# First chunk of attention and two gated MLPs: attention steps written ahead of the gates, one conversion step dropped, loads in another order

## The chip, the cores and the metric

One core of a Trainium2 chip runs the whole program. The metric is the device time of one execution in microseconds; the kernel before took 1794.08 us (median of three runs, 1793.94 to 1794.53).

## What is computed

Pooled attention feeds two MLPs:

```
k_p, v_p = mean of 8 neighbouring keys / values         # 576 -> 72
attn     = softmax(q @ k_p.T / sqrt(64)) @ v_p           # 8 batches, 8 heads, head size 64
x        = attn as [4608, 512]
x        = (sigmoid(x @ w_gate) * (x @ w_val)) @ w_out   # inner size 1536
out      = ((x @ w2_in) * cos(x @ w2_in)) @ w2_out       # inner size 2048
```

The weights arrive as float64 and are turned into two float32r parts on the chip, a high and a low one. A product of two such numbers is three matmuls: high times high, high times low, low times high.

## The kernel before

**Chunks.** The 4608 tokens are worked in nine chunks of 512. A chunk of the first stage is attention for its tokens, which gives xT (x transposed, high and low part), and then twelve blocks f = 0 to 11 of 128 gate and value columns (`gv_step`): 12 matmuls into a PSUM bank pg for the gate, 12 into pv for the value, a sigmoid on ScalarE (ACT), a product on VectorE (DVE, line 609), a store of g by DMA. After all chunks come the second product of the first MLP and the second MLP. That part, the larger, is not touched. In the code `c` is the chunk; chunk 0 is the one in which the weights are also converted.

**Order.** Every engine runs its instructions strictly in the order in which the code writes them. Nothing reorders them; the engines meet only where one waits for another's result. SyncE (SP) issues all DMAs in one queue, in order.

**Attention.** A tile of queries (up to 128 rows) goes through `q_step` (PE transposes q, ACT copies it to qT), `s_step` or, in the first half of chunk 0, `s_first` (PE multiplies with kbd, the pooled keys in block form; DVE takes the maxima mx; ACT the exponentials e and, in `s_first`, their sums sm), `normal` (DVE: a = e / sum, lines 529 to 540), `a_step` (PE transposes a into pa and par; ACT copies the high part to aT and aR; DVE subtracts for the low part, "aT low" and "aR low", line 66), and `x_step` (PE multiplies with the pooled values into px, ACT and DVE make xT's two parts). The scale 1 / (8 sqrt(64)) is put on in the exponential, and in `s_first` by an extra instruction on the negated maximum (line 512). GpSimd (POOL) pools the keys and values of the next chunk (`kv_pool`, line 362); `k_step` transposes the pooled keys into kbd, `v_step` prepares the values.

**The first chunk** is written out by hand from line 1133 on. Its four tiles are called by their first row: 0, 128, 256, 384. Its blocks 0, 1 and 2 are worked in two halves of 256 tokens: the first half while attention of the second is still under way (`gv_step(0, 0, 0)` is chunk 0, block 0, half 0), the second half at f = 0, 1, 2 of the loop in line 1244.

**Conversion.** A raw block goes through four steps: an exponent step on ACT (line 143), bit work on DVE (lines 148 and 153), the high part on ACT (line 161), the low part on DVE (line 66 with out wg or wv, "gate low", "value low"). `split()` (line 300) advances all of this by one stage for two raw tensors, a gate and a value block; the counters in `done` say how far each stage is. It only sees what has been loaded (`len(raws)`). In the first chunk `split()` stands before each block, and with two raw tensors a call the low parts of block f + 1 are made in the call before block f. Eight raw tensors (blocks 0 to 3) are loaded ahead of the loop, the other sixteen at the end of f = 0 by `load_all` (line 1274).

**The plan.** `plan(c)` spreads attention of chunk c over the twelve blocks of chunk c - 1; for chunk 1 the keys are loaded at f = 0 (line 676) and the values at f = 3 and pooled at f = 4 (lines 677 and 679). `kvraw` has two buffers, shared by keys and values, `kvrest` one.

**Banks.** PSUM tiles come from two rings of four banks, "t" and "g"; a new tile waits until the one four places before it has been read. Scores of `s_first` and the blocks share ring "g", all else uses "t".

Of the kernel before, what the change touches and what calls it, by code (L numbers as in the profile page):

```python
# [13 lines left out]
AF = mybir.ActivationFunctionType  # L14
ALU = mybir.AluOpType
# [8 lines left out]
def attention_two_mlps(  # L24
# [107 lines left out]

    def load_all():
        while len(raws) < min(len(order), len(slots) - AHEAD):
            load()
# [265 lines left out]
    def k_step(b):  # L401

        main, rest = kv["k"]
        pm = bank("t", [KM, NP, P], f"pk{b}")
        pr = bank("t", [KM, KM], f"pkr{b}")
        for i in range(NP):
            nc.tensor.transpose(pm[:, i], main[:, i], ident)
        nc.tensor.transpose(pr, rest[:KM, 0], ident[:KM, :KM])
        prv = pr.rearrange("d (i z y) -> d i z y", z=2, y=KR)
        for z in range(2):  # L410
            rows = kbds[b % 2][z * D:(z + 1) * D]
            nc.vector.tensor_copy(rows[:, :, z * KEYS:z * KEYS + KM], pm[:, :, z * KM:(z + 1) * KM])
            nc.vector.tensor_copy(rows[:, :, z * KEYS + KM:(z + 1) * KEYS], prv[:, :, z])

# [52 lines left out]
    def s_step(t):  # L467
# [4 lines left out]
        for g in range(2):  # L472
# [13 lines left out]
            half = e[:, 4 * g:4 * g + 4]  # L486
            nc.scalar.activation(half, half, AF.Exp, scale=1.0 / (POOL * math.sqrt(D)))
        sm = at.tile([rows, 16], F32, tag="sm", name=f"sm{b}_{s0}", bufs=2)[:, :H]
# [5 lines left out]
    def s_first(t, between=None):  # L494
# [7 lines left out]
        for g in range(2):  # L502
# [6 lines left out]
            m = mx[:, 4 * g:4 * g + 4]  # L509
            factor = 1.0 / (POOL * math.sqrt(D))  # L510
            nc.vector.reduce_max(out=m, in_=p, axis=AX.X)
            nc.vector.tensor_scalar(out=m, in0=m, scalar1=-factor, scalar2=None, op0=ALU.mult)
            scores.append(p)
        if between:
            between()
        for g, p in enumerate(scores):
            for h in range(4):
                n = 4 * g + h
                nc.scalar.activation(  # L519
                    e[:, n], p[:, h], AF.Exp, bias=mx[:, n:n + 1], scale=factor,  # L520
                    accum_out=sm[:, n:n + 1],
                )
# [67 lines left out]

    def gv_step(c, f, half=None):
        cols = slice(0, C) if half is None else slice(half * C // 2, (half + 1) * C // 2)
# [3 lines left out]
        for kind in "gv":  # L596
            w = block(kind, f)
            p = bank("g", [P, n], f"p{kind}{c}_{f}_{cols.start}")
            for kb in range(KB):
# [3 lines left out]
                nc.tensor.matmul(p, wl, x[:, 0, kb], start=False, stop=kb == KB - 1)  # L603
            pg.append(p)
        g = halves.pop(f, None)
        if g is None:
# [46 lines left out]
    def plan(c):  # L653
# [20 lines left out]
        if c < B:  # L674
            for g in range(3):
                (put_early if g < 2 else put)(NF - 2 if g < 2 else 0, kv_load, k, c, "k", g)
                put(3, kv_load, v, c, "v", g)
                put(1 if g == 2 or c == 1 else 0, kv_pool, c, "k", g, nc.gpsimd)
                put(4, kv_pool, c, "v", g, nc.gpsimd)
        order_ = []  # L680
# [450 lines left out]
    with tc.manual_schedule():  # L1131
# [44 lines left out]
        for n in range(2, 4):  # L1176
            stage_high(n)
        rest.append(s_first(first[3]))
        for n in range(2, 4):
            stage_low(n)  # L1180
        done.update(exponent=4, bits=4, high=4, parts=4)
        rest[2](nc.vector)
        gv_step(0, 0, 0)
        a_step(first[2])
        rest[3](nc.vector)
        split()
        gv_step(0, 1, 0)
        a_step(first[3])
        split()
        for i in range(KB):  # L1190
            x_step(0, 1, i, 1)
        split()
        gv_step(0, 2, 0)


# [25 lines left out]
        for c in range(NC):  # L1221
# [22 lines left out]
            for at_f, f in enumerate(FOLDED if c else range(NF)):  # L1244
                tick()
                if c == 0:
                    split()
                elif last:
# [25 lines left out]
                if c == 0 and at_f == 0:  # L1274
                    load_all()
                tock()
# [111 lines left out]
```

## Time and profile before

| | us |
|---|---|
| timed runs, median of 3 | 1794.08 (1793.94 to 1794.53) |
| the profiled execution | 1790.58 |
| its span, first to last instruction | 1788.6 |
| PE busy in it | 1751.2 (98%) |
| PE weight loads | 1469.0 (82%) |
| DVE busy | 1116.9 (62%) |
| ACT busy | 911.6 (51%) |
| POOL busy | 536.9 (30%) |

The shares are means over very different stages. The page's slices show PE at 9 tenths or more in all but the first two of forty, so the first 90 us are where PE has room, and it is there and a little behind it that the change lies. In the timelines below, a number in brackets at a row's end is how long the engine had been idle before that row and what ended the wait. The granted clock says at what share of its full 2.4 GHz the TensorE clock ran over a stretch; the other level is 1.2 GHz.

### The profile page before, as it was taken

What the parts mean: (1) busy time and instruction counts of PE and PEld (TensorE: products, weight loads), DVE (VectorE), ACT (ScalarE), POOL (GpSimd) and SP (SyncE); (2) the same over time, 40 slices, a digit from 0 to 9 for tenths busy, and PEclk for the clock granted to TensorE, in tenths of its full rate; (3) what the DMA queues carried; (4) which work ended last, traced back from release to release, by engine and by line L of the source; (5) the groups of instructions that cost most, each with busy time, mean ns of one, the idle gap of its engine ahead of it and who ended that gap; (6) DMA issues with size and microseconds to landing.
All of it is one profiled execution on the core that took longest, in us unless ns stands there. A gap on an engine that the chain in (4) does not pass through costs nothing. (4 is left out here: it accounts for less than half of the span.)

```text
span 1788.6 us, 24639 instructions
## 1 busy us (share of the span) xinstructions
PE 1751.2 (98%) x8560; PEld 1469.0 (82%) x8560; DVE 1116.9 (62%) x1830; ACT 911.6 (51%) x1528; POOL 536.9 (30%) x656
## 2 busy tenths in 40 slices
PE   5899999999999999999999999999999999999999
PEld 5778888888888888887888888888887878888887
DVE  7875565656565554456766765776766665655664
ACT  6654454545444453336555555565555544444443
POOL 4114444454545322220013443333334440000000
PEclk8999999999999999999999999999999999999999
DMA  9625565565866655958877778778738797666664
GB/s 270 201 72 165 190 199 183 168 183 165 251 205 210 199 193 192 338 188 277 273 252 256 260 248 262 247 248 266 257 111 289 252 330 266 216 214 212 218 218 147
DMA packets 291740, 397.47 MB, mean 222 GB/s; under 512 B 54560, under 2 KB 231200, under 8 KB 291616
## 3 DMA queue, kind: packets, MB, share of 16 engines
q1 hardware_dynamic: 291616, 395.91, 67.9%
q8 instruction: 67, 1.10, 0.3%
q14 instruction: 57, 0.47, 0.1%
HBM read 242.22 MB, written 153.62 MB: 221 GB/s over the span
## 5 line engine op out<-in xcount | busy, mean ns | idle before, releaser
L609 DVE TENSOR_TENSOR g<-pv,g 128x512 f32<-128x512 f32 (+1 forms) x111 | 75.1, 676 | 274.5 <-issue 125.2
L908 PE MATMUL ph<-x,wi 128*128 128x512 f32 x576 | 224.6, 390 | 1.9 <-DVE r L924 1.9
L909 PE MATMUL ph<-x,wi 128*128 128x512 f32 x576 | 224.3, 389 | 0.0
L910 PE MATMUL ph<-x,wi 128*128 128x512 f32 x576 | 224.1, 389 | 0.0
L914 DVE SCALAR_TENSOR_TENSOR r<-n,ph 128x512 f32<-128x512 int32 x144 | 98.9, 687 | 194.9 <-issue 87.3
L920 ACT ACTIVATE r<-r 128x512 f32<-128x512 f32 x144 | 91.2, 633 | 241.4 <-DVE r L917 98.8
L942 POOL TENSOR_TENSOR s<-r,r 128x256 f32<-128x256 f32 x64 | 75.4, 1179 | 434.9 <-DVE r L924 320.5
L66 DVE TENSOR_TENSOR sp<-sf,sp 128x1024 fp32r<-128x1024 f32 x112 | 132.8, 1229 | 80.9 <-ACT sp L998 80.9
L601 PE MATMUL pg<-xT,wg 128*128 128x512 f32 (+1 forms) x444 | 179.0, 403 | 1.8 <-ACT e L519 1.8
L603 PE MATMUL pg<-xT,wg 128*128 128x512 f32 (+1 forms) x444 | 172.4, 388 | 3.0 <-DVE wg L66 3.0
L602 PE MATMUL pg<-xT,wg 128*128 128x512 f32 (+1 forms) x444 | 172.0, 387 | 0.0
L603 PE MATMUL pv<-xT,wv 128*128 128x512 f32 (+1 forms) x444 | 170.9, 385 | 0.0
L601 PE MATMUL pv<-xT,wv 128*128 128x512 f32 (+1 forms) x444 | 170.7, 384 | 0.0
L602 PE MATMUL pv<-xT,wv 128*128 128x512 f32 (+1 forms) x444 | 170.6, 384 | 0.0
L998 ACT CAST sp<-sf 128x1024 fp32r<-128x1024 f32 x112 | 112.5, 1054 | 68.3 <-PE py_B L1101 25.0
L608 ACT ACTIVATE g<-pg 128x512 f32<-128x512 f32 (+1 forms) x111 | 65.1, 587 | 138.1 <-PE pg L603 88.4
L908 PEld LDWEIGHTS ph<-x,wi 128*128 128x128 f32 x576 | 108.3, 188 | 25.4 <-DVE r L924 2.7
L909 PEld LDWEIGHTS ph<-x,wi 128*128 128x128 f32 x576 | 108.3, 188 | 22.5
L910 PEld LDWEIGHTS ph<-x,wi 128*128 128x128 f32 x576 | 108.2, 188 | 22.5
L1096 PE MATMUL py_A<-tc,sp 128*128 128x512 f32 x384 | 120.6, 395 | 0.0
L917 DVE SCALAR_TENSOR_TENSOR r<-n,r 128x512 f32<-128x512 int32 x144 | 108.2, 751 | 5.0
L66 DVE TENSOR_TENSOR up<-uf,up 128x1024 fp32r<-128x1024 f32 x84 | 102.4, 1219 | 12.0 <-ACT up L819 12.0
(178 smaller groups left out, 4076.0 us busy)
## 6 DMA issues: line engine op xcount, KB each, us to landing
sf<-sd SPq DMA_DIRECT2D x112, 512.0 KB
so<-so SPq DMA_DIRECT2D x84, 512.0 KB
uf<-od SPq DMA_DIRECT2D x168, 256.0 KB
sd<-s SPq DMA_DIRECT2D x64, 512.0 KB
wo<-wo SPq DMA_DIRECT2D x56, 512.0 KB
od<-tg SPq DMA_DIRECT2D x48, 512.0 KB
sd<-r SPq DMA_DIRECT2D x64, 256.0 KB
raw_o<-in_moe_w_out_dram SPq DMA_DIRECT2D x28, 512.0 KB
```

Of the source, the lines that this page charges most:

```text
L66: engine.tensor_tensor(out=lo, in0=x, in1=hi.bitcast(F32), op=ALU.subtract)
L601: nc.tensor.matmul(p, wh, x[:, 0, kb], start=kb == 0, stop=False)
L602: nc.tensor.matmul(p, wh, x[:, 1, kb], start=False, stop=False)
L603: nc.tensor.matmul(p, wl, x[:, 0, kb], start=False, stop=kb == KB - 1)
L908: nc.tensor.matmul(p, wh, x[kb][:, 0], start=kb == 0, stop=False)
L909: nc.tensor.matmul(p, wh, x[kb][:, 1], start=False, stop=False)
L910: nc.tensor.matmul(p, wl, x[kb][:, 0], start=False, stop=kb == KB - 1)
L914: nc.vector.scalar_tensor_tensor(out=r, in0=n, scalar=-C1, in1=p, op0=ALU.mult, op1=ALU.add)
L917: nc.vector.scalar_tensor_tensor(out=r, in0=n, scalar=-C2, in1=r, op0=ALU.mult, op1=ALU.add)
L920: nc.scalar.activation(r, r, AF.Sin, scale=0.5)
L998: nc.scalar.copy(t[:, 0, h * w:(h + 1) * w], got[c, n, h])
L1096: nc.tensor.matmul(p, x[:, 0, m, s], w, start=fresh and m == 0, stop=False, skip_group_check=True,)
```

## The change

It has five parts.

1. The scale is multiplied into kbd when the keys are written there (`k_step`, copies become TENSOR_SCALARs); the maximum is negated by the reduction itself, so the extra instruction of `s_first` goes, and the exponentials have no scale.
2. `gv_step(..., later=True)` writes only the matmuls and returns the rest (`gated`: sigmoid and product), which the caller writes later. In the first chunk, `rest[2]` (`normal` of tile 256) stands before the low parts of block 1, `a_step` of tiles 256 and 384 before the sigmoids of blocks 0 and 1.
3. A `split()` is added at the end of the written-out part, and the `split()` at f = 5 of chunk 0 is left out.
4. The sixteen loads at the end of f = 0 are issued with the keys of chunk 1 behind the first six and the values of chunk 1 behind twelve; before, the keys stood ahead of all and the values were loaded at f = 3.
5. Chunk 1's values are pooled at f = 2 instead of f = 4.

```diff
--- before.py
+++ after.py
@@ -130,8 +130,8 @@
             raws.append(t)
         return t
 
-    def load_all():
-        while len(raws) < min(len(order), len(slots) - AHEAD):
+    def load_upto(n):
+        while len(raws) < n:
             load()
 
     def words(n, dtype, which):
@@ -409,8 +409,11 @@
         prv = pr.rearrange("d (i z y) -> d i z y", z=2, y=KR)
         for z in range(2):
             rows = kbds[b % 2][z * D:(z + 1) * D]
-            nc.vector.tensor_copy(rows[:, :, z * KEYS:z * KEYS + KM], pm[:, :, z * KM:(z + 1) * KM])
-            nc.vector.tensor_copy(rows[:, :, z * KEYS + KM:(z + 1) * KEYS], prv[:, :, z])
+            for o, i in ((rows[:, :, z * KEYS:z * KEYS + KM], pm[:, :, z * KM:(z + 1) * KM]),
+                         (rows[:, :, z * KEYS + KM:(z + 1) * KEYS], prv[:, :, z])):
+                nc.vector.tensor_scalar(
+                    out=o, in0=i, scalar1=1.0 / (POOL * math.sqrt(D)), scalar2=None, op0=ALU.mult
+                )
 
     def v_step(b, engine):
 
@@ -484,7 +487,7 @@
                 op=ALU.subtract,
             )
             half = e[:, 4 * g:4 * g + 4]
-            nc.scalar.activation(half, half, AF.Exp, scale=1.0 / (POOL * math.sqrt(D)))
+            nc.scalar.activation(half, half, AF.Exp)
         sm = at.tile([rows, 16], F32, tag="sm", name=f"sm{b}_{s0}", bufs=2)[:, :H]
         for g in range(2):
             h = slice(4 * g, 4 * g + 4)
@@ -507,9 +510,7 @@
                     x[:, 2 * g + i], kbds[b % 2][:, 2 * g + i], start=True, stop=True,
                 )
             m = mx[:, 4 * g:4 * g + 4]
-            factor = 1.0 / (POOL * math.sqrt(D))
-            nc.vector.reduce_max(out=m, in_=p, axis=AX.X)
-            nc.vector.tensor_scalar(out=m, in0=m, scalar1=-factor, scalar2=None, op0=ALU.mult)
+            nc.vector.reduce_max(out=m, in_=p, axis=AX.X, negate=True)
             scores.append(p)
         if between:
             between()
@@ -517,7 +518,7 @@
             for h in range(4):
                 n = 4 * g + h
                 nc.scalar.activation(
-                    e[:, n], p[:, h], AF.Exp, bias=mx[:, n:n + 1], scale=factor,
+                    e[:, n], p[:, h], AF.Exp, bias=mx[:, n:n + 1],
                     accum_out=sm[:, n:n + 1],
                 )
         return lambda engine: normal(t, e, sm, engine)
@@ -588,7 +589,7 @@
 
     halves = {}
 
-    def gv_step(c, f, half=None):
+    def gv_step(c, f, half=None, later=False):
         cols = slice(0, C) if half is None else slice(half * C // 2, (half + 1) * C // 2)
         n = cols.stop - cols.start
         x = xT[c][..., cols]
@@ -602,6 +603,12 @@
                 nc.tensor.matmul(p, wh, x[:, 1, kb], start=False, stop=False)
                 nc.tensor.matmul(p, wl, x[:, 0, kb], start=False, stop=kb == KB - 1)
             pg.append(p)
+        if later:
+            return lambda: gated(c, f, half, cols, pg)
+        gated(c, f, half, cols, pg)
+
+    def gated(c, f, half, cols, pg):
+
         g = halves.pop(f, None)
         if g is None:
             g = gv.tile([P, C], F32, tag="g", name=f"g{c}_{f}", bufs=4)
@@ -673,10 +680,12 @@
                 put(max(at_[n] - 3, 0), q_load, t)
         if c < B:
             for g in range(3):
-                (put_early if g < 2 else put)(NF - 2 if g < 2 else 0, kv_load, k, c, "k", g)
-                put(3, kv_load, v, c, "v", g)
+                if c > 1:
+                    (put_early if g < 2 else put)(NF - 2 if g < 2 else 0, kv_load, k, c, "k", g)
+                if c > 1:
+                    put(3, kv_load, v, c, "v", g)
                 put(1 if g == 2 or c == 1 else 0, kv_pool, c, "k", g, nc.gpsimd)
-                put(4, kv_pool, c, "v", g, nc.gpsimd)
+                put(4 if c > 1 else 2, kv_pool, c, "v", g, nc.gpsimd)
         order_ = []
         for n, t in enumerate(tiles):
             f = at_[n]
@@ -1176,21 +1185,24 @@
         for n in range(2, 4):
             stage_high(n)
         rest.append(s_first(first[3]))
+        rest[2](nc.vector)
         for n in range(2, 4):
             stage_low(n)
         done.update(exponent=4, bits=4, high=4, parts=4)
-        rest[2](nc.vector)
-        gv_step(0, 0, 0)
+        gate = gv_step(0, 0, 0, later=True)
         a_step(first[2])
         rest[3](nc.vector)
+        gate()
         split()
-        gv_step(0, 1, 0)
+        gate = gv_step(0, 1, 0, later=True)
         a_step(first[3])
+        gate()
         split()
         for i in range(KB):
             x_step(0, 1, i, 1)
         split()
         gv_step(0, 2, 0)
+        split()
 
 
 
@@ -1244,7 +1256,8 @@
             for at_f, f in enumerate(FOLDED if c else range(NF)):
                 tick()
                 if c == 0:
-                    split()
+                    if f != 5:
+                        split()
                 elif last:
                     if at_f == NF - 1:
                         pp[0].release()
@@ -1272,7 +1285,13 @@
                 for step in beside[at_f]:
                     step()
                 if c == 0 and at_f == 0:
-                    load_all()
+                    load_upto(14)
+                    for g in range(3):
+                        kv_load(k, 1, "k", g)
+                    load_upto(20)
+                    for g in range(3):
+                        kv_load(v, 1, "v", g)
+                    load_upto(len(order))
                 tock()
         while tasks:
             tick()
```

How the order of instructions changes is best seen on DVE. A row is a source line, an operation, output<-inputs and a size. First the written-out part, from the maxima of tile 384 to g of block 0; wg_405 and wv_407 are block 1's high and low parts. Before:

```order
L511 TENSOR_REDUCE mx_384_410<-psc_384_0_412 128x4
L512 TENSOR_SCALAR mx_384_410<-mx_384_410 128x4
L511 TENSOR_REDUCE mx_384_410<-psc_384_1_417 128x4
L512 TENSOR_SCALAR mx_384_410<-mx_384_410 128x4
L66 TENSOR_TENSOR wg_405<-raw_g_220,wg_405 128x512
L66 TENSOR_TENSOR wv_407<-raw_v_222,wv_407 128x512
L529 TENSOR_SCALAR sm_256_351<-sm_256_351 128x8
L532 RECIPROCAL sm_256_351<-sm_256_351 128x8
L535 TENSOR_TENSOR a_256_434<-e_256_349,sm_256_351 128x512
L540 TENSOR_TENSOR a_256_434<-e_256_349,sm_256_351 128x4x2x32
L609 TENSOR_TENSOR g_0_463<-pv_0_0_450,g_0_463 128x256
```

Here a_256 is made behind both low parts. And now (wg_399 and wv_401 are block 1):

```order
L513 TENSOR_REDUCE mx_384_404<-psc_384_0_406 128x4
L513 TENSOR_REDUCE mx_384_404<-psc_384_1_410 128x4
L530 TENSOR_SCALAR sm_256_347<-sm_256_347 128x8
L533 RECIPROCAL sm_256_347<-sm_256_347 128x8
L536 TENSOR_TENSOR a_256_424<-e_256_345,sm_256_347 128x512
L541 TENSOR_TENSOR a_256_424<-e_256_345,sm_256_347 128x4x2x32
L66 TENSOR_TENSOR wg_399<-raw_g_220,wg_399 128x512
L66 TENSOR_TENSOR wv_401<-raw_v_222,wv_401 128x512
L66 TENSOR_TENSOR aT_1_300<-pa_256_455,aT_1_300 128x4x128
L66 TENSOR_TENSOR aR_1_301<-par_256_456,aR_1_301 64x2x128
```

What moved: a_256, with the two instructions that lead to it, stands ahead of the two low parts instead of behind them, and the product g_0, which stood directly behind a_256, is further back. PE's order is the same in both kernels.

The second place is on DVE, too, at f = 5 and f = 6, from the last bit work before block 5's product to the first behind block 6's aT lows. Raw tensors are numbered as they are loaded: before, raw_g_654, 658, 662, 666 are blocks 4, 5, 6, 7. Before:

```order
L153 SCALAR_TENSOR_TENSOR raw_g_670<-raw_g_670 128x512
L153 SCALAR_TENSOR_TENSOR raw_v_672<-raw_v_672 128x512
L609 TENSOR_TENSOR g_5_1023<-pv_5_0_1010,g_5_1023 128x512
L66 TENSOR_TENSOR xT_1033<-px_0_0_0_1034,xT_1033 128x64
L66 TENSOR_TENSOR xT_1033<-px_0_1_0_1041,xT_1033 128x64
L66 TENSOR_TENSOR xT_1033<-px_0_2_0_1048,xT_1033 128x64
L66 TENSOR_TENSOR xT_1033<-px_0_3_0_1055,xT_1033 128x64
L66 TENSOR_TENSOR aT_1_1062<-pa_0_1064,aT_1_1062 128x4x128
L66 TENSOR_TENSOR aR_1_1063<-par_0_1065,aR_1_1063 64x2x128
L66 TENSOR_TENSOR wg_987<-raw_g_666,wg_987 128x512
L66 TENSOR_TENSOR wv_989<-raw_v_668,wv_989 128x512
L148 TENSOR_SCALAR raw_g_674<-raw_g_674 128x512
```

Here the low parts behind the aT lows are block 7's. And now, where raw_g_638, 642, 646, 658 are blocks 4, 5, 6, 7, from the end of tile 128's `normal` on:

```order
L541 TENSOR_TENSOR a_128_973<-e_128_954,sm_128_968 128x4x2x32
L616 TENSOR_TENSOR g_5_1003<-pv_5_0_990,g_5_1003 128x512
L66 TENSOR_TENSOR xT_1013<-px_0_0_0_1014,xT_1013 128x64
L66 TENSOR_TENSOR xT_1013<-px_0_1_0_1021,xT_1013 128x64
L66 TENSOR_TENSOR xT_1013<-px_0_2_0_1028,xT_1013 128x64
L66 TENSOR_TENSOR xT_1013<-px_0_3_0_1035,xT_1013 128x64
L66 TENSOR_TENSOR aT_1_1042<-pa_0_1044,aT_1_1042 128x4x128
L66 TENSOR_TENSOR aR_1_1043<-par_0_1045,aR_1_1043 64x2x128
L66 TENSOR_TENSOR wg_913<-raw_g_646,wg_913 128x512
L66 TENSOR_TENSOR wv_915<-raw_v_648,wv_915 128x512
L148 TENSOR_SCALAR raw_g_662<-raw_g_662 128x512
L148 TENSOR_SCALAR raw_v_664<-raw_v_664 128x512
```

What moved: in this place, the last one ahead of g of block 6, the low parts made were those of block 7 (from raw_g_666); now they are those of block 6 (wg_913, from raw_g_646). Which weights PE reads there is seen in its own order, now, at the start of block 6 (the first three products of its gate; line 604 is the one with the low part):

```order
L564 MATMUL pa_0_1044<-ident,a_0_887 128x128 x4
L564 MATMUL par_0_1045<-ident,a_0_887 128x128 x2
L602 MATMUL pg_6_0_1069<-xT_358,wg_913 128x512
L603 MATMUL pg_6_0_1069<-xT_358,wg_913 128x512
L604 MATMUL pg_6_0_1069<-xT_358,wg_913 128x512
L602 MATMUL pg_6_0_1069<-xT_358,wg_913 128x512
```

PE reads wg_913 here. The rows of PE are the same before, but for the names: there the block's weights are wg_911, whose low part DVE made before block 5's product g_5.

## Rows read from the trace of the kernel before

**Rows 1.** Windows: length, busy us by engine, granted clock, DMA share, GB/s.

```profile
37.60:50.60 13.00, 9.99 (x54) 9.03 (x54) 12.15 (x25) 8.59 (x19) 5.52 (x8) 0.77 1.10 340
...
84.60:92.10 7.50, 4.12 (x27) 3.84 (x26) 6.46 (x17) 5.59 (x12) 0.00 (x0) 0.73 0.07 26
...
98.90:121.10 22.20, 21.26 (x107) 17.08 (x106) 20.98 (x48) 15.08 (x28) 0.00 (x0) 1.00 0.16 48
...
132.50:300.00 167.50, 166.79 (x836) 139.56 (x835) 99.24 (x207) 80.98 (x141) 74.60 (x96) 1.00 0.56 176
```

**Rows 2.** PE's waits (us total, times, longest) after 132 us; before 300 us.

```profile
PE ph L908 <- DVE r L924: 1.9, 1, 1.9
...
PE pq L462 <- DMA q<-in_q_dram: 3.8, 1, 3.8
```

**Rows 3.** DVE groups by line to 60 us: busy us, mean ns.

```profile
L512 DVE TENSOR_SCALAR mx<-mx 128x4 f32<-128x4 f32 x8 | 2.4, 297 | 0.3
```

**Rows 4.** Timeline of PE: start us, us, instruction, idle before, releaser.

```profile
37.60 1.11 PE L563 MATMUL pa<-ident,a 128*128 128x128 f32 x4 [2.95 <-DVE a L535]
...
50.62 0.39 PE L603 MATMUL pg<-xT,wg 128*128 128x256 f32 x1 [2.00 <-DVE wg L66]
...
89.74 0.85 PE L584 MATMUL px<-aT,vm 128*128 128x64 f32 x3 [3.25 <-ACT qT L464]
```

**Rows 5.** Timeline of DVE, 34 to 38 us.

```profile
34.38 0.68 DVE L66 TENSOR_TENSOR wg<-raw_g,wg 128x512 fp32r<-128x512 f32 x1
...
36.02 1.53 DVE L535 TENSOR_TENSOR a<-e,sm 128x512 f32<-128x512 f32 x1
```

**Rows 6.** Timeline of POOL, 30 to 80 us.

```profile
35.74 2.39 POOL L362 TENSOR_TENSOR raw_k<-raw_k 128x512 f32<-128x512 f32 x2 [10.55 <-DMA raw_k<-in_k_dram]
```

**Rows 7.** Timeline of SP's DMA queue, 25 to 45 us.

```profile
26.11 5.51 SPq L375 DMA_DIRECT2D raw_k<-in_k_dram  x4
...
41.17 1.42 SPq L124 DMA_DIRECT2D raw_g<-in_moe_w_gate_dram  x1
```

**Rows 8.** Timeline of ACT, two stretches up to 90 us.

```profile
39.50 0.70 ACT L143 ACTIVATE raw_g<-raw_g 128x512 f32<-128x512 f32 x1
...
84.98 0.64 ACT L161 CAST wg<-raw_g 128x512 fp32r<-128x512 f32 x1
...
89.11 0.58 ACT L464 COPY qT<-pq 128x512 f32<-128x512 f32 x1
```

**Rows 9.** Timeline of DVE, 92 to 121 us (f = 6 to 9).

```profile
92.76 0.69 DVE L66 TENSOR_TENSOR aT<-pa,aT 128x512 fp32r<-128x512 f32 x1 [1.45 <-ACT aT L564]
...
93.94 0.69 DVE L66 TENSOR_TENSOR wg<-raw_g,wg 128x512 fp32r<-128x512 f32 x1
...
99.22 0.69 DVE L609 TENSOR_TENSOR g<-pv,g 128x512 f32<-128x512 f32 x1 [2.10 <-issue]
...
105.15 0.69 DVE L66 TENSOR_TENSOR wg<-raw_g,wg 128x512 fp32r<-128x512 f32 x1
...
108.35 0.69 DVE L609 TENSOR_TENSOR g<-pv,g 128x512 f32<-128x512 f32 x1
...
111.44 0.68 DVE L66 TENSOR_TENSOR wg<-raw_g,wg 128x512 fp32r<-128x512 f32 x1
...
114.52 0.69 DVE L609 TENSOR_TENSOR g<-pv,g 128x512 f32<-128x512 f32 x1
...
120.39 0.69 DVE L66 TENSOR_TENSOR wg<-raw_g,wg 128x512 fp32r<-128x512 f32 x1
```

**Rows 10.** Timeline of PE, 98 to 122 us (f = 6 to 10).

```profile
98.96 1.15 PE L475 MATMUL psc<-kbd,qT 128*128 128x144 f32 x8
...
101.06 0.40 PE L603 MATMUL pg<-xT,wg 128*128 128x512 f32 x1
...
106.17 0.46 PE L462 MATMUL pq<-ident,q 64*128 64x64 f32 x4
...
121.14 0.50 PE L603 MATMUL pg<-xT,wg 128*128 128x512 f32 x1 [0.97 <-DVE wg L66]
```


## The prediction

> **What bounds the kernel now.** I read the windows first: in each stretch, how much of it PE is busy and at which granted clock. From 132.5 us PE works 166.79 of 167.5 us at full clock, and the list of its waits after that opens with 1.9 us for one wait [rows 1, 2]. So TensorE bounds everything behind the first chunk, and nothing the change does there can be seen unless it makes PE wait. What can move the end is when PE leaves chunk 0, at about 132 us. Then I read PE's timeline up to there for the rows with an idle time in brackets. Four matter: 3.8 us for the transfer of a q tile [rows 2], 2.95 us for the attention weights a of the third tile, 2.00 us for the low part of gate block 2, and 3.25 us at f = 5 for a PSUM bank that ScalarE's copy qT frees [rows 4]. The clock is the second thing to see: 13.0 us at 0.77 behind the 2.95 us stall and 7.5 us at 0.73 around the 3.25 us stall [rows 1]. Of its two levels, 1.2 and 2.4 GHz, that is 0.23 x 13.0 = 3.0 us and 0.27 x 7.5 = 2.0 us of lost PE time; the stalls of 2.0 us and less have no such fall. Last, DVE: from 98.9 to 121.1 us it is busy 20.98 of 22.20 us, while PE is too, with 21.26 [rows 1]. PE keeps going there because the low parts it multiplies by were made one block ahead; it is caught once, for 0.97 us [rows 10]. That lead is what to watch.
>
> **The factor in the keys.** Eight L512 instructions of 0.297 us go [rows 3]. On the first two tiles ScalarE's exponentials begin some 0.3 us sooner, but PE then waits for the q transfer in both kernels, so nothing is kept; on the third and fourth tile ScalarE is busy without a break and gains about 0.1 us. The 32 copies into kbd become TENSOR_SCALARs of the same size. The trace has none of that form. From below: equal, 0. From above: 0.3 us more each (the whole of an L512), on the four of the first chunk that stand before its scores, +1.2 us; later ones lie beside PE's blocks. I take 0, since PSUM-reading DVE work elsewhere goes by its columns.
>
> **Attention ahead of the gates.** a of the third tile now stands directly behind the maxima of the fourth, before the two low parts (2 x 0.60 us, the step from 34.38 us on [rows 5]). It ran 1.53 us while POOL pooled the next keys from 35.74 us on [rows 5, 6], 9.6 us after their loads began to issue at 26.11 us; the keys are now queued behind six weight loads of 1.42 us each [rows 7], so the pooling starts near 44.3 us. a then runs beside an idle POOL, and I take 0.78 us for it (half of 1.53 and a bit; at 1.53 still the term below is 0.75 smaller). It ends at 35.2 us instead of 37.55: PE's wait falls from 2.95 to about 0.6 us, and the half clock behind it should not come (2.5 us of block 1). Block 1, 24 products of 0.12 us, then ends near 39.0 us. Part is given back. The second half's x needs the fourth tile's aT, whose copy on ScalarE now stands behind four exponent steps (39.50 us on, four of them, some 0.57 us each without their tail [rows 8]). So the copy begins at about 41.1 us, and PE's x products end near 44.9 us, where PE was done with them at 48.6 us [rows 4]. The low part of block 2, still behind two conversions and the x lows, comes at 47.5 instead of 50.6 us [rows 4]. Sum: **-3.1 us**. If PE's split wait at 40 to 43 us lowers the clock: -1; without any wait there: -5.
>
> **Loads and pooling of chunk 1.** Same bytes, other order. The keys, pooled some 9 us later than before, are wanted by PE only behind the second half of block 2. The values are pooled right behind them instead of two blocks later; DVE is loaded in both places, so I take 0 (1.5 us either way: what POOL added to the two a of the prologue, 0.75 each). Queued behind the values' loads, which wait for the key buffers, stand only the loads of blocks 10 and 11 and stores, all wanted much later. POOL's order is unchanged.
>
> **The conversion step at f = 5.** The extra split() before the loop finds only the eight blocks that are loaded; it does what the split() at f = 0 did, and that one then does nothing. The rows of the order show no instruction earlier for it. The split() at f = 5 is dropped. On ScalarE this removes two casts and two exponent steps, four of some 0.57 us from 84.98 us on = 2.3 us, ahead of the qT copy at 89.11 us [rows 8]; the 3.25 us wait shrinks to about 1.1, and the half clock there (2.5 us with its tail in block 6) should go: -4.65 us. But from f = 6 on the low parts of a block are made in its own step, directly before PE needs them. At f = 6 DVE's aT low, aR low and gate low run from 92.76 to 93.94 + 0.69 = 94.63 us, 1.87 us [rows 9], after a ScalarE copy that ends an estimated 1.15 us after the transposes begin: 3.0 us, of which PE's transposes and first two products (by the walk through f = 7 below, 2.1 us with the scores' 1.0) cover 1.1. New wait 1.9 us. Net **-2.8 us**.
>
> **The blocks 7 to 11, the term that decides.** PE's third product of a block needs the low part. DVE reaches it only after g of the block before, which needs that block's last product. So the two engines take turns.
> - f = 7: PE is through block 6 at 98.96, and would start the third product at 101.06 us [rows 10]. DVE does g at 99.22, scores, a, aT lows, and the low part from 105.15 to 105.84 us [rows 9]. In the old order that was block 8's and nobody waited; now it is block 7's. Wait: 105.90 - 101.06 = 4.8 us.
> - f = 8: block 7 ends at 106.17 us [rows 10]. With DVE free, g at +0.26, the value parts held by ScalarE's casts, the low part done at about +4.2 us; by DVE alone 0.26 + (111.44 - 108.35) + 0.68 = 4.0 [rows 9]. PE's q transposes and first two products cover 0.97. Wait 3.3 us.
> - f = 9: the chain of f = 7 with the next tile. g at +0.26 us, then 120.39 + 0.69 - 114.52 = 6.55 us to the end of the low part [rows 9]; PE covers 2.1 as at f = 7. Wait 4.75 us.
> - f = 10: g and the low part, 0.26 + 0.60 + 0.69 less 0.46: 1.15 us. f = 11: with the last aT low between, an estimate of 1.6.
>
> Sum 15.6, less the 0.97 us that goes: **+14.6 us**. DVE gets no more work; it idles in turn.
>
> **The clock.** Three of these waits are 3.3 us or longer, and the profile's stalls of 2.95, 3.25 and 3.8 us all lie in stretches with half clock. At 2.5 us each (between the 2.0 and 3.0 above): **+7.5 us**, from 0 to 9.
>
> The Trainium skill ("TensorE: Matmul & The Clock Gate", "What's actually happening") says that the slow clock is the default, that activity lifts it, and that its observation is free-running, not tied to the kernel's start. The rows agree on the first; by the last, an equal stall may be met by the gate in one execution and missed in another, which would leave +7.5 anywhere between 0 and the full amount, a rival below.
>
> **The sum.** -3.1 - 2.8 + 14.6 + 7.5 = **+16.2 us**. The profiled execution took 1790.58 us (span 1788.6), so 1806.8 by it; the three timed runs lie 3.5 us higher, at a median of 1794.08 us, and what is timed is compared with them: **1810 us**. Less than 0.2% (3.6 us) cannot be told from no change.
>
> **Rivals.**
> - *The clock stays up.* The waits come, but with PE busy on either side the gate does not fall: -5.9 + 14.6 = +8.7, 1803 us. For it: 2.00 us passed without. Against it: the three longer ones did not. 17%.
> - *The clock falls more often.* At f = 6, where transposes, small products and a 1.9 us wait lie together, and in the split wait at 40 to 43 us, too: +5, 1815 us. 17%.
> - *Faster.* The low parts do not hold PE: DVE, freed of a conversion step at f = 5, runs far enough ahead. Place: the low part of blocks 7 to 9. Price: the 14.6 and 7.5 fall away, 1794.1 - 5.9 = 1788 us. It decides once the waits from f = 7 on total under 5.9 us. For it: DVE has idle time before g at 99.22 us. Against it: that idle time is a wait for PE itself, and the low part stands behind g in DVE's order. 5%.
> - *The change doesn't do what it says, and costs nothing either:* the gains before f = 6 and the waits after cancel, 1794 us. This needs the waits at a third of what I worked out. 6%.
>
> The forecast itself has 55%. Ends: 1794.1 - 10.5 + 14.6 = 1798 (no fall of the clock, the first part at -5, no new wait at f = 5 and 6) and 1794.1 - 1.3 + 14.6 + 9 = 1816; the range is 1798 to 1817. Faster 0.05, the same 0.06, slower 0.89.
>
> **What would show it.** In the profile after: "PE pg <- DVE wg" as the largest of PE's waits, some 17 us more in total, with three rows of 3 to 5 us between about 90 and 125 us, and DVE idle before g between them; the granted clock below 1 behind each; the wait for a near 0.6 us, for qT near 1 us; PE leaving chunk 0 some 16 us later than at 132.5 us, and the rest as before. It is wrong if those pg rows are under 2 us each, or if PE is through block 11 before 132 us.

## The result: 1812 us, slower by 1.0%

| | before | after |
|---|---|---|
| timed runs, median of 4 each (us) | 1794.01 (1792.82 to 1794.53) | 1812.04 (1810.39 to 1814.35) |
| the profiled execution | 1790.58 | 1814.35 |
| its span | 1788.6 | 1812.6 |
| PE busy in it | 1751.2 | 1759.8 |
| DVE busy in it | 1116.9 | 1116.4 |

The ratio is 1.0104, with a 95% interval from 1.0092 to 1.0117. DVE does the same work as before; PE's busy time grows although it has no more products; more of them run at half clock.

The windows of after, its first three the same as in [rows 1], the fourth up to the end of chunk 0 and the last as long as the fourth of [rows 1]. Columns as there: length, busy us (and instructions) of PE, PE's weight loads, DVE, ACT and POOL, granted clock, DMA share, GB/s.

```profile
37.60:50.60 13.00, 8.79 (x60) 7.88 (x59) 10.07 (x24) 8.71 (x18) 1.87 (x2) 0.92 1.09 276
84.60:92.10 7.50, 4.78 (x27) 3.84 (x27) 6.38 (x17) 5.47 (x13) 0.00 (x0) 0.83 0.09 35
98.90:121.10 22.20, 14.23 (x51) 10.70 (x50) 14.51 (x33) 9.91 (x20) 0.00 (x0) 0.77 0.07 25
121.10:153.70 32.60, 25.59 (x104) 19.48 (x104) 13.81 (x27) 9.31 (x16) 5.65 (x6) 0.90 0.27 73
153.70:321.20 167.50, 166.92 (x837) 139.63 (x836) 100.09 (x207) 81.03 (x141) 74.73 (x94) 1.00 0.56 178
```

From 98.9 to 121.1 us PE was busy 21.26 and DVE 20.98 of 22.20 us; now it is 14.23 and 14.51, at 0.77 of full clock. DVE has not become slower at its work, and PE only where its clock is low: they take turns. Behind chunk 0 PE is full again. PE's waits, before 300 us (us in total, times, longest):

```profile
PE pg L604 <- DVE wg L66: 19.8, 8, 4.7
...
PE px L585 <- ACT qT L467: 1.2, 2, 0.8
```

The timeline of PE in after, which answers to [rows 4, 10], with the row behind each of blocks 6 to 11, so that they can be measured (start, us, instruction; in brackets the idle time before the row and what ended it):

```profile
47.31 0.39 PE L604 MATMUL pg<-xT,wg 128*128 128x256 f32 x1 [2.20 <-DVE wg L66]
...
78.69 0.50 PE L604 MATMUL pg<-xT,wg 128*128 128x512 f32 x1 [0.72 <-DVE wg L66]
...
86.47 0.52 PE L585 MATMUL px<-aT,vm 128*128 128x64 f32 x3 [0.81 <-ACT qT L467]
...
90.19 0.79 PE L604 MATMUL pg<-xT,wg 128*128 128x512 f32 x1 [1.91 <-DVE wg L66]
...
98.21 1.15 PE L478 MATMUL psc<-kbd,qT 128*128 128x144 f32 x8
...
105.13 0.79 PE L604 MATMUL pg<-xT,wg 128*128 128x512 f32 x1 [4.66 <-DVE wg L66]
...
112.61 0.46 PE L465 MATMUL pq<-ident,q 64*128 64x64 f32 x4
...
117.04 0.79 PE L604 MATMUL pg<-xT,wg 128*128 128x512 f32 x1 [3.31 <-DVE wg L66]
...
123.76 1.20 PE L478 MATMUL psc<-kbd,qT 128*64 128x144 f32 x8
...
130.54 0.79 PE L604 MATMUL pg<-xT,wg 128*128 128x512 f32 x1 [4.31 <-DVE wg L66]
...
137.24 0.39 PE L602 MATMUL pg<-xT,wg 128*128 128x512 f32 x1
...
138.84 0.50 PE L604 MATMUL pg<-xT,wg 128*128 128x512 f32 x1 [0.99 <-DVE wg L66]
...
144.06 0.58 PE L564 MATMUL pa<-ident,a 64*128 64x64 f32 x6
...
147.02 0.50 PE L604 MATMUL pg<-xT,wg 128*128 128x512 f32 x1 [1.72 <-DVE wg L66]
...
153.73 0.78 PE L585 MATMUL px<-aT,vm 128*128 128x448 f32 x3
```

Each L604 row with a bracket is the third product of a block, the first that reads a low part: blocks 2, 5, and 6 to 11. PE leaves chunk 0 at 153.73 us, 21.2 us later than at 132.50. The other side of the same turns, on DVE, which answers to [rows 3, 5, 9]. The first two rows are from the prologue: maxima without an L512 behind them, and a of tile 256 at 0.69 us where it took 1.53.

```profile
32.80 0.81 DVE L513 TENSOR_REDUCE mx<-psc 128x4 f32<-128x288 f32 x2
...
33.96 0.69 DVE L536 TENSOR_TENSOR a<-e,sm 128x512 f32<-128x512 f32 x1
...
98.46 0.69 DVE L616 TENSOR_TENSOR g<-pv,g 128x512 f32<-128x512 f32 x1 [5.84 <-issue]
...
104.39 0.69 DVE L66 TENSOR_TENSOR wg<-raw_g,wg 128x512 fp32r<-128x512 f32 x1
...
112.77 0.69 DVE L616 TENSOR_TENSOR g<-pv,g 128x512 f32<-128x512 f32 x1 [5.21 <-issue]
```

DVE idles 4.4 to 6.2 us before each g of blocks 6 to 11, since g needs PE's last product; then, in block 7, it works down its list to the gate's low part, for which PE has been waiting: 104.39 + 0.69 = 105.08 us, and PE goes on at 105.13.

### The profile page after: what moved, and what is told of

Same layout as the page of the kernel before. It is cut to its first block, busy times and chain, and to the rows that moved or that the text cites. A ratio compares the mean times of both kernels' runs of the same rounds, so it can differ in the third digit from the quotient of the medians.

```text
span 1812.6 us, 24623 instructions
## 1 busy us (share of the span) xinstructions
PE 1759.8 (97%) x8560; PEld 1472.9 (81%) x8560; DVE 1116.4 (62%) x1822; ACT 912.0 (50%) x1528; POOL 540.2 (30%) x656
## 5 line engine op out<-in xcount | busy, mean ns | idle before, releaser
L923 DVE SCALAR_TENSOR_TENSOR r<-n,ph 128x512 f32<-128x512 int32 x144 | 98.9, 687 | 197.4 <-issue 91.0
L604 PE MATMUL pg<-xT,wg 128*128 128x512 f32 (+1 forms) x444 | 177.0, 399 | 19.8 <-DVE wg L66 19.8
L602 PE MATMUL pg<-xT,wg 128*128 128x512 f32 (+1 forms) x444 | 181.6, 409 | 2.6 <-ACT e L520 2.6
L603 PE MATMUL pg<-xT,wg 128*128 128x512 f32 (+1 forms) x444 | 175.0, 394 | 0.3 <-DVE xT L66 0.3
L604 PE MATMUL pv<-xT,wv 128*128 128x512 f32 (+1 forms) x444 | 171.4, 386 | 0.0
L604 PEld LDWEIGHTS pg<-xT,wg 128*128 128x128 f32 x444 | 86.3, 194 | 40.5 <-DVE wg L66 23.0
```

The lines of the kernel that those rows point to most:

```text
L602: nc.tensor.matmul(p, wh, x[:, 0, kb], start=kb == 0, stop=False)
L603: nc.tensor.matmul(p, wh, x[:, 1, kb], start=False, stop=False)
L923: nc.vector.scalar_tensor_tensor(out=r, in0=n, scalar=-C1, in1=p, op0=ALU.mult, op1=ALU.add)
```

## The experiments

One number sums chunk 0 up: when PE starts chunk 1's x products, in before at 132.50 us. The rest of the profiled execution takes 1657.7 to 1662.1 us in all fourteen kernels, so this start decides. It is one reading of one execution of each kernel: the q transfer that PE waits for at about 20 us ends anywhere from 20.04 to 21.29 us in them, so a difference of less than about 1 us between two starts is not shown to come from the edit.

| kernel | PE leaves chunk 0, us | profiled, us | median, us | ratio to before, 95% |
|---|---|---|---|---|
| before | 132.50 | 1790.58 | 1794.01 | |
| after | 153.73 | 1814.35 | 1812.04 | 1.0092 to 1.0117 |
| 1 step put back | 130.68 | 1788.58 | 1791.71 | 0.9978 to 0.9997 |
| 2 only the step left out | 155.89 | 1813.61 | 1815.40 | 1.0106 to 1.0140 |
| 3 steps ahead of attention only | 134.68 | 1795.10 | 1793.38 | 0.9991 to 1.0009 |
| 4 the same with the loads | 130.78 | 1789.82 | 1791.20 | 0.9971 to 0.9991 |
| 5 waits filled | 146.51 | 1805.22 | 1806.37 | 1.0050 to 1.0083 |
| 6 loads first | 142.57 | 1804.15 | 1802.46 | 1.0034 to 1.0064 |
| 7 loads first, q before them | 130.68 | 1791.14 | 1791.76 | 0.9978 to 0.9996 |
| 8 low parts in the same step | 130.35 | 1789.90 | 1792.89 | 0.9983 to 1.0003 |
| 9 step at f = 5 split, low parts early | 127.39 | 1786.03 | 1786.46 | 0.9942 to 0.9975 |
| 10 step at f = 5 split, nothing else | 128.33 | 1788.33 | 1788.38 | 0.9962 to 0.9980 |
| 11 all steps split | 134.82 | 1796.90 | 1795.86 | 0.9995 to 1.0020 |
| 12 as 9, values pooled late | 127.13 | 1787.91 | 1786.13 | 0.9946 to 0.9976 |

**1. The step put back.**

```diff
-                    if f != 5:
-                        split()
+                    split()
```

> The changed kernel with the conversion step at f = 5 put back; the other parts of the change stay. Theory (the dropped step costs the lead of the low parts, and that alone makes the changed kernel slow): PE's waits for wg at f = 6 to 11 go (under 2 us in all instead of some 17), the wait for qT at f = 5 comes back at about 3 us, PE leaves chunk 0 at 129 to 131 us, and the time is 1789 to 1794 us, the first 3 us of gain ahead of block 2 being kept. Rival (the order of the loads and POOL's earlier pooling of the values cost as much as the step): the waits for wg shrink by less than half, 1800 us or more.

The only wait for wg at f = 6 to 11 is one of 0.96 us, at f = 10 where before has its 0.97; the wait for qT is back at 3.0 us. The theory came true: the dropped step is the loss. Of the 3 us of gain ahead of block 2, which it took as kept, 1.8 are left at the end of chunk 0. Its waits before 150 us:

```profile
PE px L585 <- ACT qT L467: 3.0, 1, 3.0
PE pg L604 <- DVE wg L66: 2.7, 3, 1.3
```

**2. Only the step left out** of the kernel before.

```diff
                 if c == 0:
-                    split()
+                    if f != 5:
+                        split()
```

> The kernel before with one edit: the conversion step at f = 5 is left out. Theory (this edit alone is the whole loss): waits for wg of 3 to 5 us at f = 7, 8 and 9 and the clock's falls as in the changed kernel, PE leaves chunk 0 at 152 to 156 us, 1812 to 1818 us. Rival (the loss needs the other loads or the pooling beside it): under 1803 us.

One edit makes the whole loss, with waits like those of after, 18.2 us (before 150 us):

```profile
PE pg L603 <- DVE wg L66: 18.2, 7, 4.7
```

**3. Only the attention steps written ahead, and 4. with the new loads and the pooling at f = 2.** Neither has the factor in the keys or a change to the steps.

```diff
         rest.append(s_first(first[3]))
+        rest[2](nc.vector)
...
-        rest[2](nc.vector)
-        gv_step(0, 0, 0)
+        gate = gv_step(0, 0, 0, later=True)
         a_step(first[2])
         rest[3](nc.vector)
+        gate()
```

> The kernel before with only the attention steps written ahead: normal of tile 256 ahead of block 1's low parts, the transposes of a of tiles 256 and 384 ahead of the sigmoids of blocks 0 and 1. Theory (as in the prediction): the wait for a falls from 2.95 to under 1 us if a runs beside an idle POOL, but here POOL still pools the keys of chunk 1 from about 36 us on, and a runs at 0.8 to 1.5 us; block 2 begins 2 to 3.5 us sooner; 1790 to 1792.5 us. Rival (what is gained is waited for at the next place, block 2's low part or qT at f = 5): 1793 to 1795 us.

> The kernel before with the attention steps written ahead and with the new order of chunk 1's loads and the earlier pooling of its values; without the factor in the keys and without any change to the conversion steps. Theory (the steps written ahead gain only where POOL does not pool the keys beside them: with the old loads the low part of aT of tile 256 came at 46.1 us in both): PE's x products of the second half begin at 41.5 to 42.5 us and its block 2 about 3 us sooner than before; chunk 0 is left at 129.5 to 131.5 us, 1790.5 to 1793 us, as with all but the dropped step. Rival (the gain there is the factor's): x products at 43 us or later, 1793 to 1795 us.

Alone, the steps ahead gain nothing: the third kernel's time is the rival's, and what block 1 gains is waited for already at the x products (2.28 us for an aT low), before the places that the rival named. With the loads they gain 1.7 us in chunk 0, without the factor. The timeline of DVE in kernel 3, and of POOL in it:

```profile
35.45 0.69 DVE L535 TENSOR_TENSOR a<-e,sm 128x512 f32<-128x512 f32 x1
36.06 1.50 DVE L540 TENSOR_TENSOR a<-e,sm 128x256 f32<-128x256 f32 x1
37.48 1.22 DVE L66 TENSOR_TENSOR wg<-raw_g,wg 128x512 fp32r<-128x512 f32 x1
38.62 0.94 DVE L66 TENSOR_TENSOR wv<-raw_v,wv 128x512 fp32r<-128x512 f32 x1
39.49 0.68 DVE L66 TENSOR_TENSOR aT<-pa,aT 128x512 fp32r<-128x512 f32 x1
```

```profile
35.71 2.44 POOL L362 TENSOR_TENSOR raw_k<-raw_k 128x512 f32<-128x512 f32 x2 [10.47 <-DMA raw_k<-in_k_dram]
38.23 0.79 POOL L362 TENSOR_TENSOR kS<-raw_k 128x128 f32<-128x128 f32 x1
38.98 2.57 POOL L362 TENSOR_TENSOR raw_k<-raw_k 128x512 f32<-128x512 f32 x2
```

The same instructions in kernel 4, where POOL is idle till 48.71 us:

```profile
34.40 0.69 DVE L535 TENSOR_TENSOR a<-e,sm 128x512 f32<-128x512 f32 x1
35.01 0.42 DVE L540 TENSOR_TENSOR a<-e,sm 128x256 f32<-128x256 f32 x1
35.35 0.69 DVE L66 TENSOR_TENSOR wg<-raw_g,wg 128x512 fp32r<-128x512 f32 x1
```

Beside POOL's pooling the last part of a takes 1.50 us for 0.42, and a low part 1.22 for 0.69. The last low part of a in kernel 3 then starts at 45.41 us, as in before (45.38), and PE's second x product at 46.14 (46.11). In kernel 4 that low part starts at 41.66 us. Of the 3.75 us between them 1.05 stand at the start of a already (the q transfer came 0.8 us later in kernel 3's execution); the rest goes with the stretched rows. The gain is eaten by POOL unless the keys come later, and that is what the new order of the loads is good for. Kernel 3 leaves chunk 0 2.2 us later than before though its median is the same: its profiled execution had the late transfer and a clock of 0.72 from 50 to 60 us, where before had 1.00. The subtraction from pa, which reads PSUM, took 0.68 us with POOL at work. The Trainium skill ("GPSIMD Engine Reference", "Key points") says that GpSimd shares its SBUF interfaces with VectorE and contends with VectorE instructions that have two SBUF inputs; these rows agree.

**5. The waits filled.** At f = 6, 7, 8 and 9 the first gate product is repeated 7, 18, 14 and 18 times.

```diff
+            if c == 0 and kind == "g":
+                for _ in range({6: 7, 7: 18, 8: 14, 9: 18}.get(f, 0)):
+                    nc.tensor.matmul(p, w[:, 0, :P], x[:, 0, 0], start=True, stop=True)
```

> The changed kernel with PE's waits filled: at f = 6, 7, 8 and 9 the first gate product is computed 7, 18, 14 and 18 times more, each time from the start, so the result is the same. At 0.23 us each that is 1.6, 4.1, 3.2 and 4.1 us, about as long as the waits. Theory (part of the loss is the clock, which falls around these waits because PE stands idle): with PE at work there the clock stays up from 85 to 140 us, DVE's chain is as before, PE leaves chunk 0 some 4 to 8 us sooner than at 153.7 us, 1804 to 1808 us. Rival (the waits are all of the loss and the clock adds nothing): no change, 1811 to 1814 us. Second rival (the fill delays the blocks): over 1815 us.

The turns are the same: block 7's third product starts 102.48 - 95.55 = 6.9 us after block 6's end, in after 105.13 - 98.21 = 6.9. But the clock stays up, in the windows of this kernel:

```profile
84.60:98.40 13.80, 12.70 (x74) 10.72 (x73) 9.60 (x24) 8.17 (x17) 0.00 (x0) 1.00 0.10 39
98.40:130.00 31.60, 30.61 (x138) 23.57 (x136) 21.56 (x48) 16.96 (x31) 0.00 (x0) 1.00 0.09 25
```

57 products more make the kernel 5.7 us faster than after (1806.37 against 1812.04), and chunk 0 7.2 us shorter. What the stalls cost beyond their own length is the clock, and it falls because PE stands idle.

**6. and 7. The step really sooner.** The sixteen loads go ahead of the split() at the end of the written-out part; in 7 with chunk 1's q tiles ahead of them. The step at f = 5 stays out in both.

```diff
         gv_step(0, 2, 0)
+        plans = [plan(c) for c in range(1, NC)]
+        while plans[0][1][0]:
+            plans[0][1][0].pop(0)()
+        plans[0][0][0].pop(0)()
+        load_upto(14)
...
+        load_upto(len(order))
         split()
```

(Kernel 6 has no plans lines here, and makes the q loads at f = 0.)

> The changed kernel with its sixteen loads (and those of chunk 1's keys and values between them) written ahead of the split() at the end of the hand-written part, instead of at the end of f = 0. That split() then finds blocks 4 and 5 and really is a step; the one at f = 5 stays dropped. Theory (the lead decides, not the number of steps): from f = 6 on the low parts are a block ahead again, waits for wg after f = 6 under 2 us in all; the gain ahead of block 2 (3 us) and at f = 5 (2 to 4 us) are kept; PE leaves chunk 0 at 125 to 129 us, 1785 to 1790 us. Rival (a step moved to the end of the hand-written part costs there what it saves later: four exponents ahead of the sigmoid and qT copies, raw blocks that have not landed): a new wait of over 3 us between 48 and 65 us, 1793 us or more.

> As the run before with the loads ahead of the split() at the end of the hand-written part, but with the three loads of chunk 1's q tiles that f = 0 made written ahead of the sixteen weight loads, so that SP's queue has the order of the changed kernel. Theory (the 16.9 us wait for a q tile there came only of my putting its load behind the weight loads; the lead itself is right): no wait of PE over 1.5 us after block 2, no fall of the clock from 60 us to 130 us, PE leaves chunk 0 at 123 to 126 us (the 142.6 us of that run less the 16.9 us and less 1 to 3 us of half clock behind it), 6 to 9 us sooner than in the kernel before, and 1784 to 1788 us. Rival (the earlier exponents and casts of blocks 4 and 5 hold up qT, the scores or the sigmoids of blocks 0 to 2, which that stall had covered): new waits of 3 us or more at 50 to 70 us, 1790 us or more.

Kernel 6 missed by 12 us at least. The new wait of over 3 us that its rival named is there, but for another reason: I had put a q load behind weight loads that wait for slots, and PE waited for it. Its largest wait before 150 us (the group holds one of 4.7 us at the start, too):

```profile
PE pq L465 <- DMA q<-in_q_dram: 21.5, 2, 16.9
```

Kernel 7 has no wait for wg after block 2, so the lead is right again without the step. It leaves chunk 0 at 130.68 us, not at 123 to 126: the rival came true, in part (the two waits below are of 2.06 and 3.69 us, the larger at 74 us and not at 50 to 70). PE waits twice for scores' operands that ScalarE's conversions hold up, first in the timeline of PE, then what stands before the qT copy in that of ACT:

```profile
59.84 1.20 PE L478 MATMUL psc<-kbd,qT 128*64 128x144 f32 x8 [2.06 <-ACT qT L467]
...
74.47 0.73 PE L478 MATMUL psc<-kbd,qT 128*128 128x144 f32 x4 [3.69 <-ACT raw_g L143]
```

```profile
57.99 0.68 ACT L143 ACTIVATE raw_g<-raw_g 128x512 f32<-128x512 f32 x1
58.57 0.70 ACT L143 ACTIVATE raw_v<-raw_v 128x512 f32<-128x512 f32 x1
59.14 0.39 ACT L615 ACTIVATE g<-pg 128x256 f32<-128x256 f32 x1
59.41 0.39 ACT L467 COPY qT<-pq 128x256 f32<-128x256 f32 x1
```

**8. The low parts in the same step as their casts**, the step at f = 5 still left out.

```diff
                     if f != 5:
                         split()
+                    while done["parts"] < done["high"]:
+                        stage_low(done["parts"])
+                        done["parts"] += 1
```

> The changed kernel, its conversion step at f = 5 still left out, with one edit: in every step of chunk 0 the low parts are made in the same step as the casts they belong to, behind the bit work, instead of one step later. No instruction is added; the low parts of block f + 1 come in step f again. Theory (the missing lead of the low parts is the whole loss, not the missing step): the waits for wg behind f = 6 are under 1.5 us each, the clock does not fall from 100 to 130 us, PE leaves chunk 0 at 127 to 130 us instead of 153.7, 1786 to 1790 us. Rival (DVE, which now waits for ScalarE's casts in the middle of a step, is late with g, the scores and a): two or more new waits of 2 us between 60 and 130 us, 1795 us or more.

With not one instruction more than after, PE leaves chunk 0 at 130.35 us, 23.4 us sooner. So it is the lead of the low parts that is missed, not the step. One wait is over the bound, and the clock stays up behind it, as its row in PE's timeline and the window over it (granted clock 1.00) show:

```profile
119.04 0.50 PE L604 MATMUL pg<-xT,wg 128*128 128x512 f32 x1 [2.08 <-DVE wg L66]
```

```profile
98.40:130.00 31.60, 29.02 (x136) 22.69 (x136) 23.77 (x52) 18.00 (x34) 3.31 (x4) 1.00 0.32 85
```

The start of 130.35 us is just outside the 127 to 130 that I gave, and the median of 1792.89 lies 3 us above the range (1792.87 without one execution of 4587 us); the profiled execution is one of the quickest of its ten, so what the slower ones do is not seen.

**9. to 12. The step at f = 5 in two parts.** Kernel 10: low parts first, ScalarE's part behind the attention work of f = 5.

```diff
                     if f != 5:
                         split()
+                    while f == 5 and done["parts"] < done["high"]:
+                        stage_low(done["parts"])
+                        done["parts"] += 1
...
+                if c == 0 and f == 5:
+                    split()
```

In kernel 9 the loop lacks "f == 5 and": behind every split() it makes the low parts of that step's own casts as well, which the expectation below does not say. Kernel 11 does every step in two parts, 12 is kernel 9 with chunk 1's values loaded at f = 3 and pooled at f = 4, as in before.

> The changed kernel with the conversion step at f = 5 back, but in two parts: the low parts (DVE) at its start as before, and the rest, with ScalarE's two casts and two exponents, behind the other work of f = 5 instead of ahead of it. Theory (it is DVE's low parts that PE needs, and ScalarE's part that holds up the qT copy): no waits for wg of over 1.5 us after f = 5, the wait for qT stays near 1 us, PE leaves chunk 0 2 to 5 us sooner than the 130.7 us with the step put back whole, 1786 to 1790 us. Rival (ScalarE's casts, now later, make the low parts of f = 6 or 7 late): a wait of 2 us or more there and 1791 us or more.

> The changed kernel with the conversion step at f = 5 in two parts, the low parts at its start, ScalarE's casts and exponents behind the other work of f = 5; in all other steps the low parts stay one step behind their casts (in the run before with this split they were made in the same step throughout). Theory (the place of ScalarE's part at f = 5 is what gains): waits for wg as in the kernel before (one of about 1 us at f = 9 or so), the wait for qT at 1 to 2.2 us, PE leaves chunk 0 at 127 to 129.5 us, 1786.5 to 1790 us. Rival (the gain there was the earlier low parts): waits for wg of 2 us or more at f = 6 to 9, 1791 us or more.

> As the run before it, but in every step of chunk 0: low parts at the start, casts, exponents and bit work behind the block and its attention steps. Theory (ScalarE's copies and sigmoids come first everywhere, DVE has time for the rest): no wait of PE over 1.5 us from 60 us on but that for qT, 1785 to 1789 us. Rival (the casts come so late that the low parts, first in the next step, hold up DVE and with it PE): waits for wg of 1 to 3 us at several blocks, 1792 us or more.

> The kernel with the split of the step at f = 5 and the low parts in the same step as their casts (1786.5 us), with chunk 1's values loaded at f = 3 and pooled at f = 4 as in the kernel before. Theory (the place of the values' pooling is worth 1 us at most: DVE has other work under it in both places): PE leaves chunk 0 within 1 us of 127.4 us, 1785.5 to 1788 us. Rival (pooled beside the conversion of blocks 4 and 5 it slows DVE less or more than beside f = 4's): 2 us or more either way, 1784 or 1789 us.

Kernels 9, 10 and 12 beat both kernels, before by 0.3 to 0.4% (kernels 1, 4 and 7 by 0.1 to 0.2%). Kernel 10 came as expected: the waits for wg as in before (0.96 us the largest from f = 6 on), for qT 0.8 us, a little less than expected. In kernels 9 and 12 no wait for wg is left behind block 2, and they leave chunk 0 another 1 us sooner, with a median 2 us lower. The wait for qT there is 2.2 us, not the 1 us expected. Kernel 11 is the rival: casts that late make the low parts late, 2.0 us at f = 5 and 2.1 us at f = 10. Pooling the values late moves chunk 0 by 0.26 us, which is less than these starts scatter by. The waits of kernel 12 from 50 to 300 us, where before has 3.9 us for qT and, behind block 2, 0.97 for wg:

```profile
PE px L585 <- ACT qT L467: 2.6, 2, 2.2
PE pg L603 <- DVE xT L66: 0.3, 1, 0.3
```

## Why the prediction was right

1810 us was forecast, 1812 came, and by the mechanism named: pg waiting for wg, rows of 3 to 5 us at f = 7, 8 and 9, DVE idle before g. That the two numbers lie so close is in part luck: in the trace 5.1 of the 5.9 us of gain did not come, and the medians, for reasons that stay open, differ by less than the profiled executions do.

- **The waits.** 1.9, 4.8, 3.3, 4.75, 1.15 and 1.6 us were worked out for f = 6 to 11; they measure 1.91, 4.66, 3.31, 4.31, 0.99 and 1.72. A walk through the timeline of before, with DVE's fixed order and PE's two products of cover, is good to a tenth or two, but for f = 9. Kernel 2 shows that nothing else in the change is needed for them.
- **The clock behind f = 7 to 11: right sum, by luck, of other parts.** A block takes 5.11 us from its third product to its end in before (101.06 to 106.17 [rows 10]). In after it takes 7.48, 6.72, 6.70, 5.22 and 6.71 us at f = 7 to 11: 2.4 + 1.6 + 1.6 + 0.1 + 1.6 = 7.3 us, where 7.5 was forecast as three falls of 2.5. The falls are smaller and one more: the 1.72 us wait at f = 11 has one, the 0.99 at f = 10 none. Between the ends of blocks 6 and 11 after takes 55.52 us and before 33.54, 22.0 more; 14.6 + 7.5 = 22.1 was the forecast.
- **The clock at f = 6: wrong.** The step "the half clock there should go" failed. The qT wait shrank as worked out, from 3.25 to 0.81 us, but the new wait of 1.91 us stands right behind it, and block 6 takes 8.02 us from its third product, 2.9 us of it clock. The fall moved from one wait to the other, and -2.8 became nothing: PE comes to the qT wait 0.83 us sooner than before (85.66 for 86.49 us) and ends block 6 0.75 us sooner (98.21 for 98.96). This is half of the rival in which the clock falls more often. Kernel 5 shows that this fall, too, goes when the wait is filled.
- **The prologue: right at the place, but not kept.** Block 2's third product starts at 47.31 us (47.5 forecast, 50.62 before), and the a of tile 256 takes 0.69 us (0.78). Of the 3.3 us, 1.8 are left when chunk 1's first q is transposed (54.52 for 56.32 us): the 2.20 us wait for block 2's low part has a half clock behind it that the 2.00 us of before had not. At f = 5 another 1 us goes, when DVE is late with the low parts beside POOL's pooling of the values (a bit-work row, L148, takes 1.50 us at 68.12, for 0.42 elsewhere). The wait for a, 0.6 us by forecast, is none: PE itself came later to it, at half clock behind a wait of 2.62 us for e at 31.27 us (1.84 before). So -5.9 us by block 6 came as -0.75.
- **Loads, pooling, factor.** Beside the values' pooling that 1 us goes in after, and 0.26 us in kernel 9 against 12: within the 1.5 taken as bound. The keys were pooled from 48.65 us, not 44.3. The factor was taken as 0: kernel 4, without it, leaves chunk 0 within 0.1 us of kernel 1, with it, which shows no effect above the 1 us of scatter.
- **The base.** By the profiles the change costs 23.8 us, 16.2 forecast; by the medians 18.0. The profiled execution of before is quicker than its four timed runs, that of after the slowest of its four; 2.5 us of the 23.8 lie behind chunk 0 (1660.6 against 1658.1 us), within what fourteen kernels show there. The lower end of the range took 10.5 us off for the first part at -5 and no new wait; with the -4.65 worked out at f = 5 it is 9.65, and the end 1799.

The rival *clock stays up* (1803 us) is out by the windows, *faster* and *cancels* by the 19.8 us of waits, and kernel 2 shows the edit that makes them. That the added split() is no step was read from the order, and kernel 7 shows it from the other side: given loaded blocks, the same split() restores the lead.

## What to carry to other kernels

When one stage of a hand-written pipeline is dropped or moved, follow the last product of that stage to its consumer in every later round: here a lead of zero made two busy engines, each working down its own list, take turns, and the loss came again in each round. Price a stall at its length and, if TensorE's clock falls behind it, at the products that then run at 1.2 GHz, 1.6 to 2.9 us for each stall here. To free an engine for an urgent copy, move that engine's part of the step and leave the other engine's part where its consumer needs it (kernel 10).

## What was not expected of the hardware

- Useless products made the changed kernel faster, though not as fast as before (kernel 5). The Trainium skill ("TensorE: Matmul & The Clock Gate", "What's actually happening") says that the slow clock is the default and that activity lifts it; the granted clock of 1.00 over the filled stretch, against 0.77 from 98.9 to 121.1 us in after, agrees.
- Which stalls are followed by a fall is not settled by their length alone: 2.20 us at block 2 was in after, 2.00 us was not in before, 1.72 us at f = 11 was, 2.08 us at f = 10 of kernel 8 was not. What decides between them stays open.
- POOL's additions stretched DVE instructions beside them up to 3.6 times (0.42 to 1.50 us).
